# GpSimd's local attention: 512 columns a pass in place of 256

## The chip, the cores and the metric

The kernel runs on one core of a Trainium2 chip. The metric is device microseconds (us) for one execution of the whole program. Five engines of the core work side by side, each on its own instruction stream in order: PE (TensorE, matrix products), ACT (ScalarE, exponentials), DVE (VectorE), POOL (GpSimd) and SP (SyncE, which here only issues DMAs). A step on one engine that needs a result from another waits for a semaphore.

## The reference

```python
x = A_x                                             # 2048 x 512, bf16; B_x is not used
g = _sigmoid((x * gate_w).sum(-1, keepdims=True))
a = _A_ref(x, A_wqkv, A_wo)                         # 32 heads of 16, full softmax over 2048 keys, then @ wo
b = _B_ref(x, B_wqkv, B_wo)                         # 32 heads of 16, each query sees 8 keys, then @ wo
return g * a + (1 - g) * b

# inside _B_ref
W, dil = 8, 2
idx = pos[:, None] - off[None, :]                   # off = 0, 2, .., 14
logits = jnp.einsum("bhsd,bhswd->bhsw", q, kg) * scale
logits = jnp.where(mask[None, None, :, :], logits, -1e9)
attn = _softmax(logits, axis=-1)
o = jnp.einsum("bhsw,bhswd->bhsd", attn, vg)
```

Two attentions over the same 2048 rows are mixed by a gate: A is full attention, B is local, dilated attention in which row s looks at rows s, s-2, up to s-14.

## The kernel before

**Attention A** fills ACT. Its 32 periods are (512 queries) x (group of 4 heads). In a period PE computes scores into PSUM tiles called `ring`, in sets of 3 and 2 blocks of 128 keys by 512 queries in turn; ACT takes the exponential of a whole set into `pT` (so an ACT instruction covers 1536 or 1024 columns); PE multiplies `pT` by V into an accumulator in PSUM (`misc_ps`). Two rings exist, so PE can be about one set ahead of ACT. A part of the blocks (12 of 64 in later periods) has its exponential made on DVE by integer arithmetic instead: one pass reads the scores from PSUM into `dt_a` or `wkv` and three passes make shifted copies `pd_a`.

**Attention B** runs on POOL in 16 tiles of 128 rows (`b_tile`). PE projects q, k and v, DVE evicts them, SP writes k and v to a DRAM scratch (`kv_scr`) and reads back two halves of 4 shifted copies each, `ksh` and `vsh` (128 x 4 x 512). POOL then does, for each of 4 groups of 2 shifts (`halves`):

- products `prod = ksh * qb` (`logits_mul`): per shift one pass for each `HB` columns of the 512;
- three halvings of each head's 16 products (`logits_add`, 16 to 8 to 4 to 2), where a pass takes `ws` shifts such that it covers at most `HB` sums, and a last sum into the logits `lg` (`logits_out`).

The maximum (`mx`) and the sum (`ssum`) of the softmax are DVE's, its subtraction and scaling (`lg<-lg,mx`, `lg<-lg,rr`) POOL's, its exponential ACT's. Then come POOL's products with `vsh` (`av_mul`, again `HB` columns a pass; first half into `av`, second half into `prod`), sums of these by DMAs with addition that POOL issues (`av_sum`; for the last two tiles by POOL's own passes, `av_add`), and the last sum `obb` (`av_last`). PE transposes `obb` (`fin`) for the output product.

**What sets the order.** All steps of all engines are `Op` objects. `list_schedule` replays them with a cost per step and writes out each engine's instruction order; nothing is reordered on the chip. A POOL pass of n columns is costed as a fixed part of 0.14 plus `NS[kind] * n` during which it holds a port that some DVE steps also need (`GP`, `SB`, `TT`). Some steps carry a margin after POOL's result (`SM_LAT`, `MARGIN`). Where PE would idle, the planner puts in matmuls of zeros (`zeros`, shown as `misc_ps<-z`). So when the cost of a POOL pass changes, the order of every engine is written anew. `chain_ops` writes POOL's logits steps in the order of `lseq`, which interleaves one group's halvings with the next group's products.

DVE steps that the planner lets share the port with POOL are the fills of `kt_all` (`fill`: 2048 columns in place, 512 at the start), the masks `qa` and `qt` (`ab`), and the scaled copies `vd_all` (`evd`).

Of the kernel before, what the change touches and what calls it, by code (L numbers as in the profile page):

```python
# [105 lines left out]
GP = lambda kind, n: [(False, PRE), (True, NS[kind] * n)]  # L106
# [195 lines left out]
def kernel(  # L302
# [15 lines left out]
    S, D = x2d.shape  # L318
# [71 lines left out]
    def op(eng, occ, fn, dl, **kw):  # L390
        if any(tk.kind == "misc" for tk in kw.get("use", ())):
            dl -= URG[eng]
        o = Op(eng, occ, fn, dl, **kw)
        ops.append(o)
        return o
# [3 lines left out]
    def tok(tag, cap):  # L399
        name = "banks" if tag in ("misc", "acc") else tag  # L400
        if name not in res:
            res[name] = Banks(3) if name == "banks" else Res(cap)
        return Tok(res[name], tag)
# [464 lines left out]
    for sc in range(NC):  # L868
        a = op("pe", 0.9, zmm(sc), GT + sc, full=1, deps=[o_bw, a] + o_xt[sc], alloc=[tzp] if sc == 0 else [],
               use=[tzp] if sc else [], rel=20.0)  # L870
# [6 lines left out]
    o_kvd, o_obt = [], []  # L877
    obt_tiles, obt_tok = {}, {}
    WP = WH // 2
    HB = D // 2  # L880

    def b_tile(t):
        st = {}
        tb = BT[t]
# [51 lines left out]
        tlg, tbb = tok("lg", 2), tok("obb", 1)  # L936
# [4 lines left out]
        def logits_mul(hf, wp, w_, c0):  # L941
            def s():
                if hf == 0 and wp == 0 and w_ == 0 and c0 == 0:
                    st["lg"] = work.tile([128, H, W], FP32, name="lg", tag="lg", bufs=2)
                if w_ == 0 and c0 == 0:
                    st["prod", hf, wp] = work.tile([128, WP, D], FP32, name="prod", tag="prod", bufs=NPR)
                G.tensor_tensor(out=st["prod", hf, wp][:, w_, c0:c0 + HB], in0=st["ksh", hf][:, wp + w_, c0:c0 + HB],
                                in1=st["qb"][:, c0:c0 + HB], op=ALU.mult)
            return s, "bb", HB

        def logits_add(hf, wp, n, w0, ws):
            def s():
                pv_ = st["prod", hf, wp][:].rearrange("p w (h d) -> p w h d", d=DH)
                G.tensor_tensor(out=pv_[:, w0:w0 + ws, :, 0:n], in0=pv_[:, w0:w0 + ws, :, 0:n],
                                in1=pv_[:, w0:w0 + ws, :, n:2 * n], op=ALU.add)
            return s, "ff", ws * H * n

        def logits_out(hf, wp):
            def s():
                lg = st["lg"]  # L960
                pv_ = st["prod", hf, wp][:].rearrange("p w (h d) -> p w h d", d=DH)
                w0 = hf * WH + wp
                G.tensor_tensor(out=lg[:, :, w0:w0 + WP].rearrange("p h w -> p w h"),
                                in0=pv_[:, :, :, 0], in1=pv_[:, :, :, 1], op=ALU.add)
                if hf == 1 and wp + WP == WH and t * 128 < DIL * (W - 1):
                    G.affine_select(out=lg[:], in_=lg[:], compare_op=ALU.is_ge, fill=NEG,
                                    base=t * 128, pattern=[[0, H], [-DIL, W]], channel_multiplier=1)
            return s, "ff", WP * H
# [31 lines left out]

        hn = HB // DH

        def av_mul(hf, wp, w_, c0):
            def s():
                if hf == 0:
                    o_ = av[:, wp + w_, c0:c0 + HB]
                else:
                    if w_ == 0 and c0 == 0:
                        st["av", wp] = work.tile([128, WP, D], FP32, name="prod", tag="prod", bufs=NPR)
                    o_ = st["av", wp][:, w_, c0:c0 + HB]  # L1010
                attn = st["lg"]
                w0 = hf * WH + wp + w_
                a0 = attn[:, c0 // DH:c0 // DH + hn, w0:w0 + 1]
                attn_bc = _ap(a0, [list(a0.ap[0]), [W, hn], [0, DH]])
                G.tensor_tensor(out=o_.rearrange("p (h d) -> p h d", d=DH),
                                in0=st["vsh", hf][:, wp + w_, c0:c0 + HB].rearrange("p (h d) -> p h d", d=DH),
                                in1=attn_bc, op=ALU.mult)
            return s
# [16 lines left out]
        def sums_of(wp, deps, use):  # L1035

            if t < NT - 2:
                return op("pool", DMAQ, av_sum(wp), tb + 41, deps=deps, use=use, lat=DMAQ + DMAL, far=True, name=f"B{t}")
            a_ = None
            for w_ in range(WP):  # L1040
                for c0 in range(0, D, HB):
                    a_ = op("pool", 0.0, av_add(wp, w_, c0), tb + 41, deps=deps, after=[a_], use=use, name=f"B{t}", parts=GP("ff", HB))
            return a_

        def av_last(c0):
            def s():
                if c0 == 0:
                    st["obb"] = work.tile([128, D], BF16, name="obb", tag="obb", bufs=1)
                G.tensor_tensor(out=st["obb"][:, c0:c0 + HB], in0=av[:, 0, c0:c0 + HB], in1=av[:, 1, c0:c0 + HB], op=ALU.add)
            return s  # L1050
# [25 lines left out]
        nm, na = WP * (D // HB), len(adds) + 1  # L1076
        lgs = []
        for g_, (hf, wp) in enumerate(halves):
            ps_ = mulp(logits_mul, hf, wp) + [logits_add(hf, wp, *x) for x in adds] + [logits_out(hf, wp)]
            srcs = [None] * nm + [1, 3] + list(range(nm + 1, nm + na - 1))  # L1080
            lgs.append([(g_, k_, p_, srcs[k_], ([lk[hf], qa] if k_ == 0 else [])) for k_, p_ in enumerate(ps_)])
        lseq = lgs[0][:nm]
        for g_ in range(len(halves)):
            nxt = lgs[g_ + 1][:nm] if g_ + 1 < len(halves) else []
            ad = lgs[g_][nm:]
            lseq += ad[:3] + nxt[:2] + ad[3:] + nxt[2:]
        loads["k", t], loads["v", t] = lk, lv
        l1 = chain_ops(lseq, tb - 14, {(0, 0): [tlg]}, lambda g_: [tks[g_ // (WH // WP)], tqb, tlg])
        a = op("dve", 0.34, sm_pre, tb + SMD, deps=[l1], use=[tlg])
# [12 lines left out]
        tav = tok("av", 1)  # L1102
        b, sums = None, []
        for hf, wp in halves:
            tp_ = tok("prod", NPR) if hf else None
            for n_, (w_, c0) in enumerate((w_, c0) for w_ in range(WP) for c0 in range(0, D, HB)):
                al = ([tav] if hf == wp == 0 else [tp_] if hf else []) if n_ == 0 else []
                us = [x for x in (tav, tp_) if x is not None and x not in al]
                b = op("pool", 0.0, av_mul(hf, wp, w_, c0), tb + 40, deps=[lv[hf], a], after=[b], alloc=al, use=us + [tlg, tvs[hf]],
                       name=f"B{t}", parts=GP("bf", HB))  # L1110
            if hf:
                b = sums_of(wp, [b], [tav, tp_])
                sums.append(b)
        a1 = sums_of(None, sums, [tav])
        b = op("pool", 0.0, av_last(0), tb + 43, deps=[a1], alloc=[tbb], use=[tav], name=f"B{t}", parts=GP("ff", HB))
        a1 = op("pool", 0.0, av_last(HB), tb + 43, deps=[a1], after=[b], use=[tav, tbb], name=f"B{t}", parts=GP("ff", HB))
        a1.lat += SM_LAT[3]
        tk = tok("misc", 2)
        if cb not in obt_tok:
# [15 lines left out]
    for t in range(NT):  # L1135
        b_tile(t)
# [164 lines left out]
    for k, us in enumerate(sets):  # L1301
# [14 lines left out]
        def ex(st=st, n=n, k=k):  # L1316
# [5 lines left out]
               alloc=[tr_], use=[q_tok[pi] for pi in pis], after=[last_qk[0]], scores=k % 2, name=f"qk{k}")  # L1322
# [15 lines left out]
    for pi, (c_, i) in enumerate(periods):  # L1338
# [44 lines left out]
        if i % 2 == 0:  # L1383
# [4 lines left out]
                       use=[to] + ([oat_tok[c_]] if i > 1 else []))  # L1388
# [5 lines left out]
    for t in range(NT):  # L1394
# [32 lines left out]
        for k0 in range(0, DC + nh, 2):  # L1427
            nk = min(2, DC + nh - k0)
            a = op("pe", WAVE(nk), ab_part(k0), dl - 2.0 + 0.3 * k0, full=nk,
                   deps=[a] if k0 else [o_oat[NG * c_ + ng - 1], o_wo] + o_obt[t:t + 1],  # L1430
                   alloc=[tk] if k0 == 0 else [], use=([tk] if k0 else []) + [oat_tok[c_], obt_tok[c_]])
# [4 lines left out]
        else:  # L1436
# [13 lines left out]
            b = op("pe", 0.26, tail, E2 + tt, deps=[o_oat[NP - 1], a], alloc=[tk], use=[oat_tok[c_]])  # L1450
            b = op("dve", 0.61, t_ev, E2 + 1 + tt, deps=[b, a], alloc=[tos], use=[tk])
# [47 lines left out]
```

## Time and profile before

Three runs took 814.36, 819.31 and 820.49 us, median 819.31. The profiled execution took 815.66 us, of which 813.9 is the span from the first to the last instruction.

| what | value |
|---|---|
| profiled execution, span | 815.66 us, 813.9 us |
| POOL: K products (128x256) | 256 passes, busy 175.8 us |
| POOL: halvings of 256, of 128 columns | 192 passes, 139.8 us; 64 passes, 27.3 us |
| POOL: last sum of the logits (64 columns) | 64 passes, 19.8 us |
| POOL: V products into `prod`, into `av` | 128 passes, 81.7 us; 128 passes, 79.6 us |
| POOL: `obb`; sums of the last two tiles | 32 passes, 23.1 us; 24 passes, 16.7 us |
| DVE: fills of `kt_all`, 2048 columns | 7 instructions, 9.0 us, mean 1.280 us |
| DVE: masks `qa` | 15 instructions, 7.7 us, mean 0.510 us |
| PE: matmuls of zeros | 421 instructions, 138.9 us, mean 0.386 us |

Busy time is the union of an engine's instructions, so instructions that overlap are not counted twice; a mean counts each alone. The listing of one tile or window gives start and duration of each instruction. Nearly all instructions are issued by one helper (line 364, matmuls line 373), so groups are told apart by the names of what they write and read.

### The profile page before, as it was taken

The page shows a single profiled execution, that of the slowest core. Times are in us where ns is not written, and L with a number is a line of the kernel's source. Part 1 is how long each engine was busy: PE and PEld are TensorE (multiplying, and loading weights), DVE is VectorE, ACT ScalarE, POOL GpSimd, SP SyncE. Part 2 cuts the span into 40 slices and gives each one's busy share as a digit, 9 for nine tenths or more (in the row PEclk, how much of TensorE's full clock was granted, in tenths as well). Part 3 has the DMA queues.
Part 4 walks back from the last instruction along what each step waited for, and adds up shares of the span by engine and source line. Part 5 has one row for each costly group of instructions (what it writes and reads, how often), then busy time and mean ns, then how long its engine had stood idle before and what let it go on. Part 6 is the DMA issues. An engine that isn't in the chain of part 4 may idle for free.

```text
span 813.9 us, 18012 instructions
## 1 busy us (share of the span) xinstructions
PE 751.9 (92%) x6962; PEld 246.2 (30%) x7018; DVE 690.2 (85%) x1080; ACT 785.7 (97%) x706; POOL 633.8 (78%) x1058
## 2 busy tenths in 40 slices
PE   8999999999999998999889999989989999898996
PEld 4333334324222222222222222323222222222322
DVE  5646776897887999989989899997988899898887
ACT  2999999999999999999999999999999999999995
POOL 3098969799899999999997794989769419899910
PEclk9999999999999999999999999999999999999998
DMA  7503071533544344443524407162440521522000
GB/s 261 143 2 118 2 172 50 135 86 100 132 118 112 95 114 131 103 127 93 149 55 119 126 17 171 45 162 54 91 125 12 124 92 49 147 59 72 1 2 27
DMA packets 58886, 77.22 MB, mean 95 GB/s; under 512 B 3744, under 2 KB 50848, under 8 KB 58800
## 3 DMA queue, kind: packets, MB, share of 16 engines
q1 hardware_dynamic: 52752, 54.05, 21.5%
q0 software_dynamic: 6048, 22.02, 14.6%
q8 instruction: 55, 0.90, 0.5%
q14 instruction: 31, 0.25, 0.1%
HBM read 43.78 MB, written 10.26 MB: 66 GB/s over the span
## 4 chain that ended last, share of the span: by engine, by line
ACT 46%; PE 28%; issue 18%; POOL 4%; DVE 3%; DMA 1%; SPq 0%; DVEq 0%; ACTq 0%
ACT pT L364 46%; PE misc_ps L373 19%; PE ring L373 8%; POOL prod L364 2%; POOL av L364 1%; DMA xld<-in_A_x_dram 1%; DVE kt_all L364 1%; ACT lg L364 1%; DVE pd_a L364 1%; PE pxt L622 0%; DVE wkv L364 0%; DVE osb L364 0%; POOL lg L364 0%; POOL obb L364 0%; DVE accT L364 0%
## 5 line engine op out<-in xcount | busy, mean ns | idle before, releaser
L364 ACT ACTIVATE pT<-ring 128x1536 bf16<-128x1536 f32 (+1 forms) x684 | 778.6, 1319 | 10.3 <-PE ring L373 9.8
L373 PE MATMUL ring<-qt,kt_all 32*128 32x512 bf16 x1709 | 270.4, 382 | 46.1 <-ACT pT L364 36.7
L364 POOL TENSOR_TENSOR prod<-ksh,qb 128x256 f32<-128x256 bf16 x256 | 175.8, 745 | 65.2 <-DMA ksh<-kv_scr 32.8
L373 PE MATMUL misc_ps<-pT,vp_all 128*17 128x512 bf16 (+1 forms) x1709 | 208.6, 383 | 0.1
L373 PEld LDWEIGHTS <-kt_all 32*128 32x128 bf16 x2048 | 88.4, 91 | 299.7 <-issue 290.4
L364 DVE TENSOR_SCALAR pd_a<-wkv 128x1536 uint16<-128x1536 uint16 x192 | 175.3, 941 | 1.7 <-PE misc_ps L373 0.6
L364 POOL TENSOR_TENSOR prod<-prod 128x256 f32<-128x256 f32 (+1 forms) x256 | 167.1, 668 | 5.8
L364 DVE TENSOR_SCALAR wkv<-misc_ps 128x512 uint16<-128x512 f32 x192 | 129.2, 683 | 27.9 <-PE misc_ps L373 23.1
L373 PE MATMUL misc_ps<-z 128*32 128x512 bf16 x421 | 138.9, 386 | 1.6 <-DVE z L364 1.6
L364 DVE TENSOR_SCALAR pd_a<-dt_a 128x1536 uint16<-128x1536 uint16 x147 | 135.3, 944 | 1.0
L373 PE MATMUL misc_ps<-pd_a,vd_all 128*17 128x512 bf16 x1017 | 131.3, 381 | 0.2
L373 PE MATMUL misc_ps<-qt,kt_all 32*128 32x512 bf16 x339 | 125.2, 380 | 2.4 <-DVE wkv L364 0.7
L364 DVE TENSOR_SCALAR dt_a<-misc_ps 128x512 uint16<-128x512 f32 x147 | 99.1, 685 | 18.3 <-PE misc_ps L373 16.9
L364 POOL TENSOR_TENSOR prod<-vsh,lg 128x256 f32<-128x256 bf16 x128 | 81.7, 739 | 0.0
L364 POOL TENSOR_TENSOR av<-vsh,lg 128x256 f32<-128x256 bf16 x128 | 79.6, 657 | 0.0
L373 PEld LDWEIGHTS <-vp_all 128*17 128x17 bf16 (+1 forms) x2048 | 54.7, 88 | 80.1 <-issue 66.2
L373 PE MATMUL misc_ps<-bw,xT 128*128 128x512 bf16 x164 | 50.8, 384 | 2.6 <-issue 1.1
L373 PEld LDWEIGHTS <-z 128*32 128x32 bf16 x421 | 37.0, 96 | 50.7 <-issue 28.1
L373 PEld LDWEIGHTS <-vd_all 128*17 128x17 bf16 x1017 | 35.1, 88 | 47.6 <-issue 38.0
L373 PEld LDWEIGHTS <-xT 128*128 128x128 bf16 x576 | 30.2, 99 | 33.4 <-issue 29.2
L364 POOL DMA_DIRECT2D av<-av x14 | 12.3, 882 | 33.3 <-DMA av<-prod 33.3
L373 PE MATMUL misc_ps<-xT,wkv 128*32 128x512 bf16 x384 | 37.9, 382 | 0.0
(89 smaller groups left out, 584.2 us busy)
## 6 DMA issues: line engine op xcount, KB each, us to landing
ksh<-kv_scr SPq DMA_DIRECT2D x32, 512.0 KB
vsh<-kv_scr SPq DMA_DIRECT2D x32, 512.0 KB
av<-prod POOLq DMA_DIRECT2D x28, 512.0 KB, 5.8
av<-av POOLq DMA_DIRECT2D x14, 512.0 KB, 5.0
kv_scr<-kvs SPq DMA_DIRECT2D x16, 256.0 KB
qt<-q_scr SPq DMA_DIRECT2D x30, 128.0 KB
out_dram<-osb SPq DMA_DIRECT2D x16, 128.0 KB
q_scr<-qs SPq DMA_DIRECT2D x15, 128.0 KB
```

The source lines that it names most:

```text
L364: return chain_on(key, f(*a, **k))
L373: return chain(nc.tensor.matmul(out, lhsT=lhsT, rhs=rhs, start=start, stop=stop, **kw))
```

## The change

`HB`, the columns of a POOL pass, becomes 512 in place of 256. Products, the first halving, `obb` and the last tiles' sums take one pass where they took two. Three places that counted on two passes per shift follow: the sources of the first halvings (`srcs`), the interleaving (`lseq`), and `av_last`, which is called once.

```diff
-    HB = D // 2
+    HB = D
...
-            srcs = [None] * nm + [1, 3] + list(range(nm + 1, nm + na - 1))
+            srcs = [None] * nm + [nm - 1] + list(range(nm, nm + na - 1))
...
-            lseq += ad[:3] + nxt[:2] + ad[3:] + nxt[2:]
+            lseq += ad[:1] + nxt[:1] + ad[1:2] + nxt[1:] + ad[2:]
...
-        b = op("pool", 0.0, av_last(0), tb + 43, deps=[a1], alloc=[tbb], use=[tav], name=f"B{t}", parts=GP("ff", HB))
-        a1 = op("pool", 0.0, av_last(HB), tb + 43, deps=[a1], after=[b], use=[tav, tbb], name=f"B{t}", parts=GP("ff", HB))
+        a1 = op("pool", 0.0, av_last(0), tb + 43, deps=[a1], alloc=[tbb], use=[tav], name=f"B{t}", parts=GP("ff", HB))
```

## The prediction

> **What bounds the kernel now.** First the busy times by engine, then the same in stretches.
>
> ```profile
> PE 751.9 (92%) x6962; PEld 246.2 (30%) x7018; DVE 690.2 (85%) x1080; ACT 785.7 (97%) x706; POOL 633.8 (78%) x1058
> ```
>
> ```profile
> 19.60:50.00 30.40, 28.18 (x366) 10.90 (x367) 17.45 (x34) 30.15 (x28) 9.97 (x16) 1.00 0.38 96
> 50.00:100.00 50.00, 47.17 (x526) 17.75 (x527) 31.37 (x56) 49.10 (x45) 45.49 (x76) 1.00 0.15 49
> 100.00:210.00 110.00, 103.95 (x1060) 38.06 (x1066) 87.61 (x152) 106.82 (x97) 91.03 (x145) 0.98 0.44 109
> 210.00:350.00 140.00, 132.07 (x1098) 39.77 (x1111) 128.36 (x189) 139.23 (x125) 133.56 (x224) 1.00 0.44 111
> 350.00:805.00 455.00, 421.69 (x3685) 129.39 (x3710) 410.49 (x599) 454.88 (x410) 346.68 (x581) 1.00 0.33 85
> ```
>
> After the window and its length stand the busy times of PE, weight loads, DVE, ACT and POOL, then PE's granted clock. ACT's column carries the argument: from its first exponential (19.6) to its last (805) it is idle for 0.25 + 0.90 + 3.18 + 0.77 + 0.12 = 5.2 us. The chain of waits says the same (46% ACT, 28% PE). So 785.4 of the 813.9 us of span are a stream of exponentials that this change doesn't touch, with 5.2 us of holes. Next, what ACT waits for in those holes, and who waits for POOL:
>
> ```profile
> POOL av L364 <- DMA av<-prod: 33.3, 11, 9.1
> POOL prod L364 <- DMA ksh<-kv_scr: 32.8, 4, 16.8
> ...
> ACT pT L364 <- PE ring L373: 9.8, 11, 5.1
> ...
> PEld L1127 <- POOL prod L364: 1.9, 7, 0.4
> ```
>
> The 5.1 is the wait for the first exponential; the rest is PE late with scores. ACT has no wait put down to POOL; PE waits for POOL 1.9 us in all, at the transposes of `obb`. POOL itself waits for DMAs. The lead-in (19.6) and the tail (8.8) hold none of the passes changed: the first K product starts at 39.8, the last `obb` ends at 775.5.
>
> **What a 512 pass costs.** The halvings give a ladder of busy time per pass: 64 columns 19.8/64 = 0.309, 128 columns 27.3/64 = 0.427, 256 columns 139.8/192 = 0.728. The last step is 0.301/128 = 2.35 ns a column. At that slope 512 take 0.728 + 256 x 0.00235 = 1.330, and the pair replaced 1.456: 0.126 saved. At the lower slope (0.118/64 = 1.84 ns) it is 1.199, saving 0.257; if the slope steepens again by the same 1.28 (3.0 ns), 1.496, a loss of 0.04. I take 0.126, the nearest row. K products (0.687), V products (161.3/256 = 0.630) and `obb` (0.722) have no ladder and get the same. Pairs merged: 128 K products, 64 halvings, 128 V products, 16 `obb`, 12 of the last tiles' sums: 348. POOL saves 348 x 0.126 = 44 us (ends -14 and 89), 2.7 us a tile, and falls from 634 to 590. [...]
>
> On the path this is worth at most the 1.9 us that PE waits for POOL, and less on ACT, which has a set in hand; I take 0. What POOL saves goes into its waits for `av<-prod` and `ksh`. The margin that hides POOL is thin in places: in one tile the subtraction ends 0.9 us before ACT turns to that tile's exponential (below), in another `obb` ends at 602.3 and its transposes start at 602.8.
>
> ```profile
> 598.94 0.63 POOL L364 TENSOR_TENSOR lg<-lg,mx 128x256 f32<-128x256 f32 x1
> ...
> 600.44 0.50 ACT L364 ACTIVATE lg<-lg 128x256 f32<-128x256 f32 x1
> ```
>
> **The order written anew.** The instruction orders of the two programs show the same DMAs on SP (177, the `vsh` and `ksh` loads and some output stores some places earlier or later) and the same 42 DMAs on POOL; POOL's instructions fall from 1063 to 715. ACT's 16 logits exponentials stand on average 3 places earlier, about 3.5 us at 1.13 us a place, `obb`'s transposes up to 35 score matmuls earlier. PE has 396 matmuls of zeros for 421: 25 x 0.386 = 9.7 us less PE work, off the path. B's steps thus move forward, some across 210 us, from where ACT loses 0.2 to 0.5% to where it lost 3%. A shift of 10 us is a fifth of a tile's pace (about 49 us), so a fifth of its 12 projection matmuls, 1 us of PE. Cost between 0 and 1 us; I take 0.5.
>
> **DVE behind longer passes.** The trace shows DVE steps that wait for POOL's pass to end:
>
> ```profile
> 152.07 2.89 DVE L364 TENSOR_SCALAR kt_all<-kt_all,rowc,negk 128x2048 bf16<-128x2048 bf16 x1
> ```
>
> ```profile
> 151.67 2.73 POOL L364 TENSOR_TENSOR prod<-vsh,lg 128x256 f32<-128x256 bf16 x4
> ```
>
> ```profile
> L364 DVE TENSOR_SCALAR qa<-qs x15: 282/446/1175, 22.2 to 731.4; 128x256 uint32<-128x256 uint32 x15
> ```
>
> A fill takes 0.803 with POOL quiet (at 208.44); this one took 2.89 and finished only after all four passes. The 7 fills lose 7 x (1.280 - 0.803) = 3.3 us to this, the 15 masks 15 x (0.510 - 0.282) = 3.4 (duration here is min/median/max). The three-shift copies `pd_a` don't wait: 886 to 955 ns for all 339. A pass twice as long is met as often by time, and has twice as much left: between +0 (the run of passes is as long as before) and +7 us of DVE; I take +7. Behind a waiting fill DVE holds up its own evictions from PSUM, and PE waits for those. How much reaches ACT: the worst wait, 2.1 us at 152, lies in the stretch 150 to 200, where ACT was idle 0.48 us in all, so at most 0.23 of it. 7 x 0.23 = 1.6 us.
>
> [...]
>
> **Sum.** 815.66 - 0 + 0.5 + 1.6 = 817.8 for an execution like the profiled one. The runs' median lies 3.65 above that execution, so in their terms 819.31 + 2.1 = 821.4.
>
> **Rivals.** A measurement of this kernel tells about 1% (8.2 us) from no change.
>
> *The lock decides (0.17).* All of DVE's added wait reaches ACT, and more: a run of 512 passes keeps a fill or mask out as it did at 152, in the stretch before 210 us where PE is 94% busy and has no time to catch up. For: 11 of the 31 steps that may need the port lie at 72 to 210 us. Against: steps do get in between passes mostly (the median mask waits 0.16). Price: 7 us at full weight; with two more waits like that at 152, doubled (2 x 4.2), 15: 826 to 835. It passes 1% from 8.2 us on, half or more of its cases.
>
> *POOL falls behind its written-out place (0.08).* The order counts on 0.14 saved per merged pair. If 512 columns take twice 256, POOL is 348 x 0.14 = 49 us, 3.0 a tile, slower than planned. The exponential with 0.9 us in hand then waits 2.1, the transposes with 0.5, 2.7 and 2.8 in hand hold PE 2.5, 0.3 and 0.2: 5 us, 826. For: the margins; against: the ladder.
>
> *PE loses its clock (0.05).* Fewer zeros leave PE more idle. In 140 to 150 us the granted clock was 0.84, and ACT idled 1.08 us there and 0.87 in the 10 us before: 2.0 a dip. Four more dips make 8, at the 1% bound: 828. Against: one dip in the 785 us now.
>
> *A gain (0.10).* B off PE's and POOL's way closes the holes: at most 5.2 us, 814.1, under 1%. Beyond it a median run near 811 would need the fast end of the runs (814.36) and the holes closed: 0.04.
>
> **How the numbers follow.** The forecast, ACT-bound with up to 3 us of new holes, has 0.60 and lies at 819 to 824. Slower by over 1%: 0.17 x 0.6 + 0.08 x 0.4 + 0.05 x 0.5, and 0.02 for the forecast, 0.18. Faster by over 1%: 0.04. Within: 0.78. The range reaches down to the gain with the runs' spread, 813, and up to the middle of the lock's cases, 831.
>
> **What would show it.** Right: ACT idle between its first and last exponential under 10 us, no ACT wait on POOL, K products at 1.2 to 1.35 a pass, POOL near 590 busy, masks with a mean near 0.7 and a largest one over 1.5. The lock: ACT's holes before 210 us grow past 8, behind fills. Lag: ACT waits put down to `lg` on POOL. Clock: PE's clock under 1.00 in more than one stretch. I'm wrong outright if passes of 512 take over 1.5 us or the new order leaves holes in ACT after 350 us, where there are none now.

## The result, and the profile after

The changed kernel takes 819.67 us (median of 20 runs, 817.28 to 822.96) against 817.17 for the kernel before (20 runs, 814.24 to 820.49): ratio 1.0033, interval 1.0019 to 1.0048. It is slower by 2.5 us in the medians (1.6 to 3.9 by the interval), well under 1%. The profiled execution took 818.65 us with a span of 816.9, 3.0 longer than before.

The busy times, then the same stretches as before (window, its length, busy PE, weight loads, DVE, ACT, POOL, then PE's granted clock):

```profile
PE 753.2 (92%) x6937; PEld 245.3 (30%) x6993; DVE 688.4 (84%) x1080; ACT 786.7 (96%) x706; POOL 581.0 (71%) x710
```

```profile
19.60:50.00 30.40, 28.18 (x369) 10.93 (x373) 18.32 (x34) 30.15 (x28) 10.53 (x11) 1.00 0.34 96
50.00:100.00 50.00, 47.63 (x514) 18.25 (x511) 33.40 (x61) 49.12 (x45) 43.34 (x55) 1.00 0.15 49
100.00:210.00 110.00, 104.47 (x1082) 38.44 (x1089) 87.30 (x151) 107.18 (x97) 87.79 (x104) 1.00 0.47 114
210.00:350.00 140.00, 132.07 (x1083) 38.52 (x1093) 123.17 (x183) 139.59 (x126) 123.52 (x153) 1.00 0.42 106
350.00:805.00 455.00, 419.06 (x3633) 127.69 (x3661) 408.17 (x599) 452.06 (x406) 308.82 (x374) 0.99 0.34 85
```

POOL does 52.8 us less, and none of it reaches the end. As before, ACT's column carries the reading. Its holes are now 0.25 + 0.88 + 2.82 + 0.41 + 2.94 = 7.3 us, 2.1 more than before, and its busy time is 1.0 more. Together that is the 3.0 us of span. In this execution the new holes lie after 350 us, where there were 0.12.

Who waits for whom (total us, times, longest):

```profile
POOL av L364 <- DMA av<-prod: 36.9, 10, 5.1
POOL prod L364 <- DMA ksh<-kv_scr: 35.7, 5, 26.0
...
ACT pT L364 <- PE ring L373: 8.7, 10, 5.1
...
ACT pT L364 <- PE misc_ps L373: 2.7, 3, 2.0
```

ACT still waits for PE alone. Not in the list before is the second kind of wait, for `misc_ps`, of which one is 2.0 us long. And the passes themselves, by shape:

```profile
L364 POOL TENSOR_TENSOR prod<-ksh,qb 128x512 f32<-128x512 bf16 x128 | 151.3, 1196 | 70.8 <-DMA ksh<-kv_scr 35.7 <-DVE qb L364 18.0 <-DVE wkv L364 6.3
L364 POOL TENSOR_TENSOR prod<-prod 128x512 f32<-128x512 f32 x64 | 82.8, 1294 | 1.0
L364 POOL TENSOR_TENSOR prod<-vsh,lg 128x512 f32<-128x512 bf16 x64 | 73.6, 1214 | 0.0
L364 POOL TENSOR_TENSOR av<-vsh,lg 128x512 f32<-128x512 bf16 x64 | 68.4, 1099 | 0.2
```

A pass of 512 costs 151.3/128 = 1.18 us for K, 82.8/64 = 1.29 for the halving, 142.0/128 = 1.11 for V, so the pairs save 0.19, 0.16 and 0.15 us.

### The profile page after: what moved, and what is told of

The parts are those of the page before. It is cut to its first block, busy times and chain, and to the rows that moved or that the text cites. A ratio compares the mean times of both kernels' runs of the same rounds, so it can differ in the third digit from the quotient of the medians.

```text
span 816.9 us, 17616 instructions
## 1 busy us (share of the span) xinstructions
PE 753.2 (92%) x6937; PEld 245.3 (30%) x6993; DVE 688.4 (84%) x1080; ACT 786.7 (96%) x706; POOL 581.0 (71%) x710
## 4 chain that ended last, share of the span: by engine, by line
ACT 48%; PE 27%; issue 20%; DVE 3%; DMA 1%; POOL 1%; SPq 0%; DVEq 0%; ACTq 0%
ACT pT L364 47%; PE misc_ps L373 19%; PE ring L373 8%; DMA xld<-in_A_x_dram 1%; ACT lg L364 1%; DVE wkv L364 1%; POOL prod L364 1%; DVE pd_a L364 1%; PE pxt L622 0%; DVE dt_a L364 0%; DVE osb L364 0%; DVE accT L364 0%; DVE oat L364 0%; DVE kt_all L364 0%; ACT xT L364 0%
## 5 line engine op out<-in xcount | busy, mean ns | idle before, releaser
L364 POOL TENSOR_TENSOR prod<-ksh,qb 128x512 f32<-128x512 bf16 x128 | 151.3, 1196 | 70.8 <-DMA ksh<-kv_scr 35.7
L364 POOL TENSOR_TENSOR prod<-prod 128x512 f32<-128x512 f32 (+2 forms) x192 | 158.9, 828 | 3.5
L373 PE MATMUL misc_ps<-pd_a,vd_all 128*17 128x512 bf16 x1017 | 133.2, 382 | 0.2
L373 PE MATMUL misc_ps<-z 128*32 128x512 bf16 x396 | 130.6, 389 | 1.7 <-DVE z L364 1.6
L364 POOL TENSOR_TENSOR prod<-vsh,lg 128x512 f32<-128x512 bf16 x64 | 73.6, 1214 | 0.0
L364 POOL TENSOR_TENSOR av<-vsh,lg 128x512 f32<-128x512 bf16 x64 | 68.4, 1099 | 0.2
L373 PEld LDWEIGHTS <-z 128*32 128x32 bf16 x396 | 34.2, 96 | 47.6 <-issue 27.1
L364 DVE TENSOR_SCALAR_CACHE_REDUCE kt_all<-misc_ps,rowc 128x512 bf16<-128x512 f32 x32 | 23.8, 745 | 17.5 <-PE misc_ps L373 17.0
```

Of the source, the lines that this page charges most:

```text
L364: return chain_on(key, f(*a, **k))
L373: return chain(nc.tensor.matmul(out, lhsT=lhsT, rhs=rhs, start=start, stop=stop, **kw))
```

## The experiments

Two things changed at once: the passes on POOL, and the order that the planner wrote for every engine. The theories to tell apart were **passes** (longer POOL passes keep out the DVE steps that the planner lets share the port with POOL, and that reaches ACT) and **order** (the new order of PE, DVE and ACT has worse waits written into it). Since instructions are fixed by the order, each half of the change can be run with the other half undone. All ratios are to the kernel before, run beside.

**new_again** is the changed kernel once more, as a yardstick.

> The changed kernel once more, beside the others of this set. Both theories: 1.0033 of before (1.002 to 1.005).

Measured: 818.51 us, 1.0028 (1.0012 to 1.0044). The effect repeats. ACT's holes in its profiled execution are 8.8 us and lie elsewhere: 3.79 between 210 and 350 us, 1.01 after 350.

**old_order_512**: the order of before on PE, DVE, ACT and SP, instruction for instruction; on POOL the first of each pair issues nothing and the second issues the pass of 512. The edit, shown for the K products, is the same for halvings, V products, sums and `obb`:

```diff
-                G.tensor_tensor(out=st["prod", hf, wp][:, w_, c0:c0 + HB], in0=st["ksh", hf][:, wp + w_, c0:c0 + HB],
-                                in1=st["qb"][:, c0:c0 + HB], op=ALU.mult)
+                if c0:
+                    G.tensor_tensor(out=st["prod", hf, wp][:, w_, :], in0=st["ksh", hf][:, wp + w_, :],
+                                    in1=st["qb"][:], op=ALU.mult)
```

> The instruction order of before on PE, DVE, ACT and SP, with the changed kernel's POOL passes of 512 columns in the place of the second of each pair. Theory 'order': equal to before, 0.999 to 1.001, ACT idle about 5 us in its stream. Theory 'passes': as slow as the changed kernel, 1.002 to 1.005. POOL busy about 581 in either.

Measured: 816.3 us, 0.9996 (0.9980 to 1.0013), with POOL at 586.5 us busy. In the old order the passes of 512 cost nothing that can be measured; the changed kernel's 1.0033, and the 1.0028 run beside, lie outside this interval. ACT's idle time came out at about 9 us in its stream and not the 5 expected. The profiled execution was this kernel's slowest (820.02), and the granted clock was under 1.00 in three stretches of 10 us (0.83, 0.66 and 0.83, from 80, 140 and 320 us); the median is what decides. The fills and masks, two of DVE's kinds of step that the planner puts at the port, were not held longer either (count, busy us, mean ns, idle before):

```profile
L364 DVE TENSOR_SCALAR qa<-qs 128x256 uint32<-128x256 uint32 x15 | 8.4, 560 | 0.1
L364 DVE TENSOR_SCALAR kt_all<-kt_all,rowc,negk 128x2048 bf16<-128x2048 bf16 x7 | 8.2, 1173 | 0.1
```

With the floors of the prediction (0.282 and 0.803) the masks lose 15 x 0.278 = 4.2 us and the fills 7 x 0.370 = 2.6: 6.8 us, against 3.4 + 3.3 = 6.7 before. The sum is the same. The third kind, the copies `vd_all`, isn't in it: they took 9.8 us in this execution and 7.8 before. All of DVE's steps that the planner puts there took 28.9 us against 27.0 here, and 26.2 against 27.5 in the second order tested below (old_plan_0.12_512 and old_plan_0.12_again), so no direction shows.

**new_order_256**: the changed kernel's order on every engine, each pass of 512 issued as two of 256 at its place:

```diff
+                for c in (0, D // 2):
+                    G.tensor_tensor(out=st["prod", hf, wp][:, w_, c:c + D // 2], in0=st["ksh", hf][:, wp + w_, c:c + D // 2],
+                                    in1=st["qb"][:, c:c + D // 2], op=ALU.mult)
```

> The changed kernel's instruction order on every engine, but each merged POOL pass issued as two passes of 256 at the same place. Theory 'order' (the new order of PE, DVE and ACT costs the time): as slow as the changed kernel, 1.002 to 1.005 of before. Theory 'passes' (longer POOL passes keep DVE from the shared port, which holds up PE and then ACT): back at before, 0.999 to 1.001. POOL busy 50 us more than in the changed kernel (about 631) in either.

Measured: 839.12 us, 1.0266 (1.0242 to 1.0289), POOL 630.3 us busy. Neither theory expected this. POOL is 49 us busier here than its order allows for, so the run doesn't tell the theories apart. It shows that the new order does not merely hold its own holes: it relies on the faster POOL. ACT in this kernel (start, duration, idle before and its releaser):

```profile
204.82 1.49 ACT L364 ACTIVATE pT<-ring 128x1536 bf16<-128x1536 f32 x1
208.26 3.28 ACT L364 ACTIVATE pT<-ring 128x1024 bf16<-128x1024 f32 x3 [1.95 <-PE misc_ps L373]
218.36 2.37 ACT L364 ACTIVATE pT<-ring 128x1536 bf16<-128x1536 f32 x2 [6.82 <-PE ring L373]
```

The 6.82 us follow from one DVE step, seen in DVE's timeline, while POOL ran passes of 256:

```profile
206.85 0.68 DVE L364 CAST vp_all<-misc_ps 128x512 bf16<-128x512 f32 x1
207.45 8.28 DVE L364 TENSOR_SCALAR kt_all<-kt_all,rowc,negk 128x2048 bf16<-128x2048 bf16 x1
215.65 0.94 DVE L364 TENSOR_SCALAR pd_a<-dt_a 128x1536 uint16<-128x1536 uint16 x1
```

```profile
206.17 2.81 POOL L364 TENSOR_TENSOR prod<-ksh,qb 128x256 f32<-128x256 bf16 x4
208.68 1.64 POOL L364 TENSOR_TENSOR prod<-prod 128x256 f32<-128x256 f32 x2
210.04 1.52 POOL L364 TENSOR_TENSOR prod<-ksh,qb 128x256 f32<-128x256 bf16 x2
```

A fill that takes 0.80 us with POOL quiet was kept out for 7.5 us, while eleven more passes began, one after another. That POOL leaves no gap does not explain it. In new_again the same fill met passes of 512 that left none either:

```profile
204.99 1.75 DVE L364 TENSOR_SCALAR kt_all<-kt_all,rowc,negk 128x2048 bf16<-128x2048 bf16 x1
```

```profile
205.04 1.16 POOL L364 TENSOR_TENSOR prod<-ksh,qb 128x512 f32<-128x512 bf16 x1
206.15 1.18 POOL L364 TENSOR_TENSOR prod<-prod 128x256 f32<-128x256 f32 x1
```

It got in behind the first of these. Here the two records overlap by 0.05 us (205.04 + 1.16 against 206.15); at 207 us the records of neighbouring passes overlap by 0.24 to 0.30. This was counted over all 13 traces, from the start and duration of each record, for fills and masks held 0.1 us or more over their floor and for boundaries from 0.13 us after their start on. They were passed over at 37 of the 38 boundaries where two passes overlap by 0.2 us or more, and got in at all 102 where the overlap is less than 0.1. Every run of such overlapping passes begins behind a DMA that POOL issues. In the old order the overlapping boundaries are 91 with passes of 256 and 23 with 512 (old_order_512), and the longest such run falls from 4.3 us to 2.6. Why records overlap by so much is open.

In new_order_256, `pd_a` waited behind the fill on DVE, and PE waited 6.4 us for `pd_a`. A mask at 245.40 took 5.50 us in the same way, and ACT lost 4.07 us behind it. A third hole, 2.98 at 512, has another cause: there PE waits 2.8 us for POOL's `obb`, which is late. How the 22 us divide between lockout and lateness was not tried.

**The order written anew with nothing else changed.** Four kernels differ from before or from the changed kernel by the planner's fixed cost of a POOL pass alone:

```diff
-PRE = 0.14
+PRE = 0.12
```

> The kernel before with passes of 256, but the planner's fixed cost of a POOL pass is 0.16 in place of 0.14, so that the order is written anew with nothing else changed. Theory 'order': any such re-planning moves the time by some tenths of a per cent, 0.997 to 1.005, not equal to before. Theory 'passes': 0.999 to 1.001, since passes are as before.

> The kernel before, passes of 256, the planner's fixed cost 0.12. Theory 'order': anywhere between 0.998 and 1.006 of before; with four such orders (two of 512 passes, two of 256), the two groups overlap. Theory 'passes': 0.999 to 1.001.

> The changed kernel, passes of 512, the planner's fixed cost of a POOL pass 0.12 in place of 0.14: another order for the same passes. Theory 'order': anywhere between 0.998 and 1.006 of before, not tied to the changed kernel's 1.003. Theory 'passes': 1.002 to 1.004.

> The same with 0.16. Theory 'order': anywhere between 0.998 and 1.006 of before. Theory 'passes': 1.002 to 1.004.

| passes | planner's 0.12 | 0.14 | 0.16 |
|---|---|---|---|
| 256 | 0.9985 (0.9968 to 1.0001) | 1 (before) | 1.0048 (1.0026 to 1.0069) |
| 512 | 1.0022 (1.0003 to 1.0042) | 1.0033 (1.0019 to 1.0048) | 1.0011 (0.9989 to 1.0033) |

A constant that changes no pass costs 0.5% with passes of 256, more than the change under study. The rows overlap, so 0.33% is of the size that a new order can make. Whether orders made for 512 are worse on the whole, three in a row don't decide; all three lie above 1. Part of what an order costs is which fill or mask meets a run of POOL's passes: in old_plan_0.16's profiled execution a mask at 158.84 us took 2.81, PE waited 1.8 behind it and ACT lost 1.29 at 163.64.

**old_plan_0.12_512** and **old_plan_0.12_again** repeat the test of the passes in a second order, and ask whether that order beats before.

> The order of old_plan_0.12 on every engine, with POOL passes of 512 columns in it. Theory 'order': equal to old_plan_0.12, 0.997 to 1.001 of before. Theory 'passes': 1.002 or 1.003 slower than old_plan_0.12.

> old_plan_0.12 once more: is it faster than before, or the same? 0.9985 of before if it is real, 1.000 if not.

Measured: 815.57 us, 0.9996 (0.9983 to 1.0009) with 512, and 815.76, 1.0005 (0.9988 to 1.0022) with 256. In this order too the width of the passes makes no difference that can be measured, and the order is no faster than before. No version run here beats the kernel before.

**new_v_first** asks whether the holes are written into the order. In both profiled executions of the changed kernel ACT has a hole of 1.95 us at 204 us; here the first one, then DVE and PE at that place:

```profile
201.66 2.40 ACT L364 ACTIVATE pT<-ring 128x1024 bf16<-128x1024 f32 x2
206.01 2.37 ACT L364 ACTIVATE pT<-ring 128x1024 bf16<-128x1024 f32 x2 [1.95 <-PE misc_ps L373]
```

```profile
203.74 0.94 DVE L364 TENSOR_SCALAR pd_a<-dt_a 128x1536 uint16<-128x1536 uint16 x1
204.60 0.68 DVE L364 CAST vp_all<-misc_ps 128x512 bf16<-128x512 f32 x1
```

```profile
202.88 0.39 PE L373 MATMUL ring<-qt,kt_all 32*128 32x512 bf16 x2
...
205.34 1.00 PE L373 MATMUL misc_ps<-pT,vp_all 128*17 128x512 bf16 x12
```

ACT's scores were there at 203.3. What it lacked was a free `pT` buffer: twelve products of `pT` with V stood back until DVE had evicted the last part of V (204.60 + 0.68 = 205.28), which the new order has behind two `pd_a` passes. The edit takes one of these passes, and PE's product of it, to behind the eviction and the twelve products:

```diff
     order = list_schedule(ops, zeros)
+    ev, = [o for o in order if o.name == "vpe24.8"]
...
+    order.insert(order.index(ev) + 1, sh)
+    k = order.index(lo) + 1
+    order[k:k] = [zs[0], dp, zs[1]]
```

> The changed kernel with one step of the new order moved: DVE evicts the last V projection (into vp_all) ahead of one three-shift pass, and PE's products of pT with it go ahead of the products of that pass. Theory 'written-in holes' (the new order contains fixed waits, above all the 1.95 us hole of ACT at 204 us, where pT times V waits for this eviction): the hole shrinks to about 1.2 us, since the eviction can start 0.75 us earlier, and the rest of the order stays; time 0.999 of the changed kernel, too little to be told by the time alone. Theory 'it is the clock dips alone': the hole stays at 1.95.

Measured: the hole is 1.30 us, as expected; 819.59 us, 1.0023 (1.0003 to 1.0043), which can't be told from the changed kernel. So the place of one eviction makes at least 0.65 us of this hole, and the hole is the order's.

**new_more_zeros** asks for the share of PE's clock. In the changed kernel's first execution the holes after 350 us lie where the granted clock falls (columns as in the stretches above, the clock being the third figure from the end):

```profile
515.00:525.00 10.00, 8.41 (x79) 2.72 (x73) 8.21 (x13) 10.00 (x10) 9.54 (x13) 1.00 0.19 44
525.00:535.00 10.00, 9.85 (x72) 2.38 (x72) 7.71 (x12) 8.83 (x8) 3.43 (x5) 0.83 0.76 148
535.00:545.00 10.00, 9.63 (x91) 2.85 (x89) 9.93 (x15) 10.00 (x11) 3.63 (x4) 1.00 0.70 202
545.00:555.00 10.00, 8.28 (x71) 2.44 (x64) 8.30 (x15) 9.25 (x10) 9.22 (x13) 0.83 0.20 57
```

PE is busy 8.4 of 10 us in the first of these, the clock is 0.83 in the next, and ACT loses 1.17 us there and 0.75 in the last. In the second execution (new_again) these two dips are absent and another, 0.72 from 235 to 245 us, goes with 2.42 us of holes. This one follows a mask that took 2.43 us (DVE, then PE):

```profile
234.99 2.43 DVE L364 TENSOR_SCALAR qa<-qs 128x256 uint32<-128x256 uint32 x1
237.34 0.68 DVE L364 CAST kvs<-misc_ps 128x512 bf16<-128x512 f32 x1
```

```profile
238.07 0.37 PE L373 MATMUL misc_ps<-qt,kt_all 32*128 32x512 bf16 x1 [1.00 <-DVE kvs L364]
```

The mask waited behind two overlapping passes of 512, DVE's next eviction came late, PE idled 1.00 us for it, the granted clock then was 0.60 from 239 to 241 us and 0.50 to 245, and ACT lost 3.4 us in four holes up to 247. In the first execution the same mask took 0.48 us, the clock there stayed at 1.00, and ACT lost nothing. So a DVE wait behind passes of 512 seems to have reached ACT in the new order; that one step led to the next is read from the two traces, not tried. Such dips differ between the two executions of the changed kernel, and the hole at 204 is in both. The old order, though, has one at 140 to 150 us in both of its executions (0.84 before, 0.66 in old_order_512).

The run asks whether more matmuls of zeros help against the dips:

```diff
-            for _ in range(n):
+            for _ in range(n + 1):
                 mm(tz[0:32, :], z32[:], z_bc, True, True, tile_position=(0, 0))
```

> The changed kernel's order, with one matmul of zeros more at each place that has some (558 in place of 396). If dips of PE's clock are a part of the new order's loss, they get fewer and the time falls to 0.998 to 1.000 of the changed kernel; if the zeros stand in PE's way instead, ACT waits longer for scores and the time is 1.000 to 1.01 of it.

Measured: 835.34 us, 1.0243 (1.0223 to 1.0264). The mean clock rose from 0.993 to 0.996, and ACT's holes grew: its waits for `misc_ps` went from 3 (2.7 us) to 12.

```profile
ACT pT L364 <- PE ring L373: 13.3, 25, 5.1
...
ACT pT L364 <- PE misc_ps L373: 6.4, 12, 2.4
```

The 162 added matmuls stand in the way of PE's real work: from 19.6 to 805 us PE is busy 743.6 us where it was 731.4, and ACT 768.1 where it was 778.1. The run doesn't price the dips: whatever it won on the clock it lost, and much more, on PE's time.

The clock of every execution, which is on record, says more. Its mean is 0.9954 over the 82 runs of the kernel before that stand beside these experiments, and 0.9938 over the changed kernel's 32; the mean times are 816.7 and 819.2 us. A straight line of time against clock falls by 6.6 and 6.0 us for each 0.01, and at a clock of 0.995 the two lines stand at 817.0 and 818.5. So 1.5 of the 2.5 us are there at the same clock, and about 1 us goes with the lower clock. This is a correlation, not an experiment.

## Why the prediction was right, and where its sum was not

The total was right: +0.26% forecast (821.4 on 819.31), +0.33% measured, within 1%, slower. Two of its terms were wrong, by 2.0 us too little and 1.6 too much, and that these nearly cancel was luck.

- *ACT sets the end, POOL's gain is worth nothing.* Right. POOL's 52.8 us went into idle time; in its own waits above, the DMA waits alone hold 72.6 us where they held 66.1. Zero was the right value: with the passes of 512 in the old order, POOL does 47.3 us less and the time is the same.
- *A pass of 512.* The ladder gave 1.330 for the halving, measured 1.294, and 44 us for POOL, measured 52.8: the halving itself saved 0.16 where 0.126 was taken, the V products 0.15 and the K products 0.19. K products at 1.18 lie just under the 1.2 to 1.35 named as a sign of being right.
- *DVE behind longer passes, 7 us of DVE and 1.6 on ACT.* This step failed where it was tested, in the old orders. The measured value there is 0: 0.9996 in one order, 0.9996 against 0.9985 and 1.0005 in another, and the wait of fills and masks summed to 6.8 us where it was 6.7. "Has twice as much left" counts one pass for each wait. The longest waits are not of that kind: a DVE step can be passed over by a whole run of overlapping passes, as the fill of 8.28 us was, and as the prediction's own fill at 152 us was, which four passes kept out. With 512 columns the longest such run in the old order is shorter, not longer (2.6 us for 4.3). How the short waits and the long ones balance was not taken apart. The other end of the bracket (+0) was in the prediction and was not taken. In the new order no run takes the passes apart from their order, and there the way from a mask to ACT exists, as the two traces at 235 us suggest. The masks' mean, forecast at 0.7 with a largest over 1.5, was 0.42 (largest 1.25) in the first execution and 0.63 (2.43) in the second.
- *The order written anew, 0.5 us.* This is the term that was mis-sized, 0.5 for 2.5: the passes cost nothing in the old order, so what the change costs comes with the new one. Of the place, half was right. The hole that is in both executions, at 204 us, lies in the crowded stretch before 210 us that the prediction named. But what makes it is where an eviction of A's V stands, and no run ties that to B's steps having moved. ACT's holes in that stretch don't measure it (3.18 before, 2.82 after): the 3.18 hold the dip at 140 to 150 us, which the prediction put at 2.0, and the changed kernel has none there. What the prediction gave as proof that it would be wrong outright, holes after 350 us, is there in the first execution (2.94 us) and weaker in the second (1.01). Most of the 2.94 lies beside clock dips. Of ACT's idle spells, those that have the same length in both profiled executions of an order, added up from its timelines, are 3.7 us in the old order and 5.4 in the new, so 1.7 of the 2.5 us. By subtraction that leaves about 1 us for what comes and goes, dips above all, as much as the clocks on record give; no run shows it.
- *The lock, as a rival* (a run of POOL's passes keeps a fill or mask out). It doesn't decide here, but such a wait is in the traces: at 207 us in new_order_256 a fill of 0.80 us took 8.28, and ACT had a hole of 6.8 us behind it. It came where POOL was 5 to 7 us behind its place (the tile's K products start at 206.17, against 199.13 and 201.20 in the changed kernel) and ran with overlapping passes of 256. POOL's next pass went ahead of the waiting fill eleven times over.
- *POOL behind its written-out place.* Priced at 5 us; when POOL really was that much behind (new_order_256 against new_again), it cost about 20 (1.0266 against 1.0028). The margins were counted, and one of the three long holes is of that kind (2.98 at 512 us); the lockout of DVE by a late POOL was not.
- *PE's clock.* Right in kind: holes of 0.75 to 3.4 us beside each dip (granted clock 0.83 and 0.83 in the first execution, 0.72 in the second). Four more in the whole span were not reached in either execution of the changed kernel.

## What to carry to other kernels

Where a planner writes the order, a changed cost re-plans every engine, and that alone moved the time by up to 0.5% here: before crediting a small loss to the edit, run the new instructions in the old order and the old ones in the new. An engine off the path can still hold another up: here a fill of 0.80 us was kept out for 7.5 us while eleven passes of POOL, whose records overlap, began one after another, and ACT had a hole of 6.8 us behind it. Look for what the other engine has to do there. An order that counts on a faster engine can lose far more when that speed is missing (2.4% here) than it cost in itself. A hole of the same length in two executions (1.95 us at 204 us here, with a clock of 1.00 from 200 to 206 us in the first) is likely to be in the order; for one that comes and goes, look at the clock and at the waits before it.

## What the runs showed of the hardware that was not expected

A fill and a mask of DVE were passed over by POOL's passes many times in a row in new_order_256: the fill of 0.80 us took 8.28, the mask of 0.28 took 5.50, behind passes that began 0.62 to 0.68 us apart and whose records are 0.86 to 0.99 us long. In all 13 traces the fills and masks held 0.1 us or more over their floor got in where neighbouring records overlap by less than 0.1 us (102 of 102 boundaries) and were passed over where these overlap by 0.2 or more (37 of 38), and every run of such passes begins behind a DMA issue of POOL. POOL's passes did not get cheaper alike: 256 more columns cost 0.49 us for the K product (1.18 for 0.69), 0.48 for the V product (1.11 for 0.63) and 0.57 for the halving (1.29 for 0.73).
